# Attention and a maxout layer on one Trainium2 core: W2 Wo accumulated in two halves at the head, and attention moved from two batches ahead to one

## The chip, the cores and the metric

The kernel runs on one core of one Trainium2 chip. The metric is the device time of that core in microseconds (us).

## The reference, cut to what matters

```python
B, H, S, Ns, D = (8, 8, 512, 32, 64)          # d_model 512, d_ff 1024
a      = softmax(scale * x @ state.T)         # 512 tokens attend to 32 states
xread  = a @ state
a2     = softmax(scale * state @ x.T)         # 32 states attend to 512 tokens
sread  = a2 @ x
x      = concat([xread, sread])               # (8 * 544, 512)
out    = maximum(x @ w1, x @ w2) @ w_out
```

The kernels use three identities. `xread @ W` is `a @ (state @ W)`, so each batch multiplies its states into the weights once ("SW") and layer 1 contracts over the states instead of over the model dimension. `max(h1, h2)` is `h2 + relu(h1 - h2)`, so layer 1 needs only W1 - W2 and a ReLU. The term `h2 @ Wo` is `a @ (state @ (W2 Wo))`; so the product W2 Wo (512 x 512) is formed once. In the names of tiles, xt is x transposed, aT is a transposed, sr is the sread of one batch (the "state rows", whose own layers run for all batches near the end; sread_t collects them transposed), r is a ReLU's output and ob a batch's output.

## The kernel before

One batch in the steady loop is layer 1 (16 matmuls and 8 ReLUs), then layer 2 (4 chunks of 10 matmuls); the attention of a later batch is put as "fillers" between the chunks. Slots 8 to 11 are the places behind chunks 0 to 3 of layer 2.

```python
LEAD = 2
xio  = ctx.enter_context(tc.tile_pool(name="xio", bufs=3))
keep = ctx.enter_context(tc.tile_pool(name="keep", bufs=LEAD + 1))
psum = ctx.enter_context(tc.tile_pool(name="ps", bufs=8, space=bass.MemoryType.PSUM))
# ... loads on the SP queue: states, x0, x1, W2 and W1 in halves, x2, states, x3; Wo on GpSimd

def l2(b, fill):
    # ...
    for c in range(NC):
        # ... 10 matmuls into one PSUM bank: 2 with aT (SW), 8 with r (Wo)
        copy("A" if c % 2 else "V", ob[:, c, :], p)
        # ...
        run(*fill.get(NF + c, ()))
    if b < B - 1:
        nc.sync.dma_start(out=dst, in_=ob)          # the 1 MB output, after the last filler

def fillers(b):
    # ...
    n = b + LEAD
    if n < B:
        put(8, lambda: u_sc(n, 0))                  # scores, exp, norm
        put(9, lambda: u_sc(n, 1))
    # ... compact_x(n + 1), u_sw(b + 1)
    if n < B:
        put(10, lambda: u_sr(n))
        put(11, lambda: d_at(n), lambda: u_srt(n))  # d_at: transposing DMA into aT
    if n + 1 < B:
        put(11, lambda: d_xt(n + 1))                # transposing DMA into xt
```

At the head, attention and layer 1 of batches 0 and 1 run interleaved while the weights arrive; W2 Wo comes after them, in one piece:

```python
def w_wo(i):
    p = bank()
    for f in range(NF):
        nc.tensor.matmul(p, w2t[:, i, f, :], wo[:, f, :], start=(f == 0), stop=(f == NF - 1))
    negate("A", wcat[:, i, FF:WC], p)
```

The softmax here doesn't subtract the row's maximum and nothing guards it: scores larger than these inputs give would overflow.

## Time and profile before

| | before |
|---|---|
| time, median of 3 runs | 163.75 us (163.23 to 164.83) |
| span of the profiled run | 161.7 us |
| TensorE (PE) busy | 145.4 us, 90% |
| start of layer 2 of batch 0 | 47.09 us |
| one batch of the loop | 14.32 us |
| mean granted clock of TensorE | 0.996 |

The page's rows of digits cut the span into 40 slices of some 4 us; a digit is the busy share in tenths. The prediction shows those rows, the chain of waits and one batch of the loop. Two further lines of the page are needed later: the granted clock of TensorE by slice, and the group of W2 Wo (busy us, mean ns of one matmul, then PE's idle time ahead of the group).

```profile
PEclk9999999999999999999999999999999999999998
...
L350 PE MATMUL ps<-wo,w2t 128*128 128x512 bf16 x32 | 7.1, 379 | 0.0
```

The first six nines of the clock row are not a measurement: the packed trace (the file that is kept of the profiled run) holds no clock record before 23.96 us, and the page shows time without a record as full. Five warm-up matmuls take 2.31 us there, 0.4 us each or more, against 0.22 for one of W2 Wo, so PE was cold. The mean clocks in the tables suffer from the same and are not compared.

A 512-column matmul is recorded with 379 ns though its successors start every 216 ns: records of matmuls overlap. Hence a gap in brackets before a group is some 0.16 us shorter than the time that PE really lost. Sums of lost time have this 0.16 added for each gap.

### The profile page before, as it was taken

Reading aid. Unit: us, or ns where it says so; the run is one execution under the profiler, and the core shown is the slowest. Engines: PE = TensorE matmul, PEld = TensorE weight load, DVE = VectorE, ACT = ScalarE, POOL = GpSimd, SP = SyncE. Lnnn points to the kernel's source line nnn. Section 1 sums busy time; section 2 is a strip of 40 time slices with the busy share of each in tenths; the row PEclk is TensorE's granted clock in tenths of the full one; section 3 lists DMA queues with packets and bytes.
Section 4 is the critical chain, followed back from the end, with each engine's and each line's share of the span. In section 5 each row is a group of like instructions: output and inputs, shape, how many; then the busy total and the mean of one; then the engine's idle time right before and its main releaser. Section 6 shows DMA issues by size and latency. Waiting matters only on the chain.

```text
span 161.7 us, 3207 instructions
## 1 busy us (share of the span) xinstructions
PE 145.4 (90%) x1349; PEld 72.0 (45%) x1349; DVE 87.0 (54%) x150; ACT 77.9 (48%) x130; POOL 37.1 (23%) x41
## 2 busy tenths in 40 slices
PE   6267389499999999999999999999999999999990
PEld 2255245354544444444445444444444444744430
DVE  5457638799594257355565645556564533416110
ACT  3154955759437166538365743837254243307001
POOL 3140299431002725202702520220130000000000
PEclk9999999999999999999999999999999999999998
DMA  4999999920862796995399096039104400613131
GB/s 111 352 384 386 381 317 196 256 94 2 157 232 47 152 298 225 227 302 191 85 305 303 26 183 271 4 68 315 71 4 130 195 0 4 259 38 92 65 129 67
DMA packets 34365, 27.98 MB, mean 173 GB/s; under 512 B 21424, under 2 KB 30640, under 8 KB 33456
## 3 DMA queue, kind: packets, MB, share of 16 engines
q1 hardware_dynamic: 33312, 26.74, 54.7%
q0 software_dynamic: 1040, 1.05, 4.1%
q8 instruction: 10, 0.16, 0.4%
q14 instruction: 3, 0.02, 0.1%
HBM read 15.20 MB, written 8.91 MB: 149 GB/s over the span
## 4 chain that ended last, share of the span: by engine, by line
PE 85%; DVE 7%; DMA 3%; ACT 2%; issue 1%; SPq 0%
PE ps L292 43%; PE ps L277 17%; PE ps L350 4%; PE ps L239 4%; PE ps L181 3%; DMA xf<-in_x_dram 3%; PE ps L306 2%; PE ps L316 2%; PE ps L204 2%; PE ps L163 2%; PE ps L252 2%; DVE w1b L60 2%; DVE sbd L60 1%; DVE es L188 1%; PE ps L314 1%; PE ps L222 1%
## 5 line engine op out<-in xcount | busy, mean ns | idle before, releaser
L292 PE MATMUL ps<-wo,r 128*128 128x512 bf16 x256 | 60.5, 379 | 0.0
L292 PEld LDWEIGHTS <-r 128*128 128x128 bf16 x256 | 24.8, 98 | 29.7 <-issue 0.4
L267 DVE TENSOR_SCALAR r<-ps 128x512 bf16<-128x512 f32 x32 | 22.1, 691 | 17.3 <-PE ps L277 17.2
L191 POOL TENSOR_TENSOR a<-e,er 128x512 bf16<-128x512 bf16 x14 | 15.1, 1080 | 70.7 <-DVE er L190 35.6
L277 PE MATMUL ps<-aT,swt 128*128 128x512 bf16 x128 | 29.4, 380 | 0.3 <-ACT swt L58 0.3
L58 ACT COPY ob<-ps 128x512 f32<-128x512 f32 x16 | 9.4, 585 | 28.0 <-PE ps L292 24.8
L265 ACT ACTIVATE r<-ps 128x512 bf16<-128x512 f32 x32 | 19.2, 600 | 7.4 <-PE ps L277 7.0
L60 DVE COPY ob<-ps 128x512 f32<-128x512 f32 x16 | 11.1, 692 | 18.7 <-PE ps L292 18.6
L58 ACT CAST swt<-ps 128x512 bf16<-128x512 f32 x24 | 13.9, 588 | 11.8 <-PE ps L239 9.7
L292 PE MATMUL ps<-swt,aT 128*128 128x512 bf16 x64 | 19.1, 382 | 0.3 <-DVE swt L60 0.3
L277 PEld LDWEIGHTS <-swt 128*128 128x128 bf16 x128 | 12.1, 98 | 14.6 <-issue 0.6
L184 ACT ACTIVATE e<-ps 128x512 bf16<-128x512 f32 x16 | 9.6, 600 | 18.4 <-PE ps L181 16.3
L60 DVE CAST swt<-ps 128x512 bf16<-128x512 f32 x24 | 15.7, 661 | 4.9 <-PE ps L252 3.2
L188 DVE TENSOR_REDUCE es<-e 128x16 f32<-128x512 bf16 x16 | 10.9, 682 | 12.4 <-ACT e L184 12.4
L62 POOL CAST xp<-xf 128x2048 bf16<-128x2048 f32 (+1 forms) x9 | 13.6, 1516 | 12.3 <-DMA xf<-in_x_dram 12.2
L58 ACT CAST xc<-xf 128x1024 bf16<-128x1024 f32 x12 | 12.4, 1048 | 0.0
L181 PE MATMUL ps<-sbd,xt 128*128 128x64 bf16 x128 | 7.2, 205 | 2.2 <-ACT xt L58 1.1
L181 PEld LDWEIGHTS <-xt 128*128 128x128 bf16 x128 | 6.2, 105 | 5.8 <-DVE xt L60 1.4
L239 PE MATMUL ps<-wcat,sbd 64*32 64x512 bf16 x160 | 8.1, 386 | 0.0
L292 PEld LDWEIGHTS <-aT 128*128 128x128 bf16 x64 | 4.7, 97 | 7.0 <-issue 3.8
L350 PE MATMUL ps<-wo,w2t 128*128 128x512 bf16 x32 | 7.1, 379 | 0.0
L252 PE MATMUL ps<-w1b,sbd 64*32 64x256 bf16 x64 | 2.6, 338 | 4.4 <-DVE w1b L60 4.4
(60 smaller groups left out, 113.4 us busy)
## 6 DMA issues: line engine op xcount, KB each, us to landing
xf<-in_x_dram SPq DMA_DIRECT2D x7, 1024.0 KB, 7.9
out_dram<-ob SPq DMA_DIRECT2D x7, 1024.0 KB, 4.9
w2f<-in_moe_w_dram SPq DMA_DIRECT2D x2, 1024.0 KB, 11.2
w1f<-in_moe_w_dram SPq DMA_DIRECT2D x2, 1024.0 KB, 12.8
xf<-in_x_dram SPq DMA_DIRECT2D x2, 512.0 KB, 5.0
wo<-in_moe_w_out_dram POOLq DMA_DIRECT2D x1, 1024.0 KB, 12.5
out_dram<-ob SPq DMA_DIRECT2D x4, 256.0 KB, 2.0
out_dram<-obs SPq DMA_DIRECT2D x8, 64.0 KB, 1.7
```

The lines of the kernel that those rows point to most:

```text
L58: nc.scalar.copy(o, i)
L60: nc.vector.tensor_copy(o, i)
L62: nc.gpsimd.tensor_copy(o, i)
L181: nc.tensor.matmul(p[:, k * 64:k * 64 + 64], d["xt"][:, 4 * i + 2 * g + cp, :], sbd[:, b, 2 * i + g].rearrange("p u n -> p (u n)"), start= ...
L188: nc.vector.tensor_reduce(d["es"][:, g], d["e"][:, g].rearrange("p i c n -> p (i c) n"), axis=mybir.AxisListType.X, op=ALU.add)
L191: mul.tensor_mul(d["a"][:, g].rearrange("p c i n -> p i c n"), d["e"][:, g], d["er"][:, g].rearrange("p (i c) -> p i c", i=4).unsqueeze(3) ...
L239: nc.tensor.matmul(pg[g][32 * i:32 * i + 32, :], sbd[64 * g:64 * g + 64, b, 2 * i + g, g, :], wcat[64 * g:64 * g + 64, i, ch * 512:(ch + 1 ...
L265: nc.scalar.activation(out=o, in_=p, func=ACTF.Relu)
L267: nc.vector.tensor_scalar(o, p, scalar1=0.0, scalar2=None, op0=ALU.max)
L277: nc.tensor.matmul(p, SW[b][:, g, f * 128:(f + 1) * 128], AT[b][:, g, :], start=(g == 0), stop=(g == 1))
L292: nc.tensor.matmul(p, w, v, start=(k == 0), stop=(k == NF + 1))
L350: nc.tensor.matmul(p, w2t[:, i, f, :], wo[:, f, :], start=(f == 0), stop=(f == NF - 1))
```

## The change

The intent: form W2 Wo in the head, where PE idles and DMA is full, instead of in the full stretch; make layer 2 of batch 0 in two passes as Wo's halves arrive; and keep less in SBUF and PSUM by running attention one batch ahead. The diff, cut to its core:

```diff
-    LEAD = 2
+    TWO = 3
-    xio = ctx.enter_context(tc.tile_pool(name="xio", bufs=3))
+    xio = ctx.enter_context(tc.tile_pool(name="xio", bufs=2))
-    keep = ctx.enter_context(tc.tile_pool(name="keep", bufs=LEAD + 1))
+    keep = ctx.enter_context(tc.tile_pool(name="keep", bufs=2))
-    psum = ctx.enter_context(tc.tile_pool(name="ps", bufs=8, space=bass.MemoryType.PSUM))
+    psum = ctx.enter_context(tc.tile_pool(name="ps", bufs=4, space=bass.MemoryType.PSUM))
+    accs = ctx.enter_context(tc.tile_pool(name="acc", bufs=4, space=bass.MemoryType.PSUM))
 ... loads
-    load_states(first); load_x(0, 2); load_x(1); W2 and W1 by halves; x2; states; x3
+    load_w(w2f, moe_w2, 0)
+    load_wo(0)
+    load_states(first)
+    load_x(0)
+    load_w(w2f, moe_w2, 1)
+    load_wo(1)
+    load_w(w1f, moe_w1, 0)
+    load_w(w1f, moe_w1, 1)
+    load_x(1)
+    ... the other states; x2
 ... layer 2
+    def l2_close(b, c):
+        copy("A" if c % 2 else "V", ob[:, c, :], OB[b][1 + c])
+        if b == B - 1:
+            nc.sync.dma_start(out=dst[:, c:c + 1], in_=ob[:, c:c + 1])
+        elif c == NC - 1:
+            nc.sync.dma_start(out=dst, in_=ob)
     def l2(b, fill):
         for c in range(NC):
-            ... 10 matmuls and a copy
+            l2_open(b, c)
+            l2_add(b, c, range(NF))
+            l2_close(b, c)
             run(*fill.get(NF + c, ()))
-        if b < B - 1:
-            nc.sync.dma_start(out=dst, in_=ob)
 ... W2 Wo
+    def w_wo(ch, i):
+        if ch == 0:
+            WO[i] = acc()
+        for f in range(4 * ch, 4 * ch + 4):
+            nc.tensor.matmul(WO[i], w2t[:, i, f, :], wo[:, f, :], start=(f == 0), stop=(f == NF - 1))
+        if ch:
+            copy("A" if i % 2 else "V", wcat[:, i, FF:WC], WO[i])
 ... fillers
-        n = b + LEAD
+        n = b + 1
-            put(10, lambda: u_sr(n))
-            put(11, lambda: d_at(n), lambda: u_srt(n))
+            put(10, lambda: u_sr(n), lambda: d_at(n))
+            put(11, lambda: u_srt(n))
 ... head (abridged)
+    warm_up(9); W2 half 1 cast and transposed; Wo half 1 cast; W2 Wo half 1 for rows 0, 1
+    states, their negation, cast of x0; W2 Wo half 1 for rows 2, 3; attention of batch 0
+    W2 half 2 cast and transposed; Wo half 2 cast; W2 Wo half 2 for all rows
+    SW and layer 1 of batch 0; layer 2 of batch 0 over f 0..3, later over f 4..7, batch 1 between
+    state copies and W1 - W2 moved into layer 2 of batch 1
```

The 1 MB output was issued after the last filler, and is now issued inside `l2_close`, ahead of it. The last filler issues the transposing DMA into xt on the same SP queue.

More of the change, by code (lines that the diff above doesn't have):

```diff
@@ L54, in bank, with acc @@
         return psum.tile([128, 512 if dtype == F32 else 1024], dtype, tag="ps", name="ps")
+    def acc():
+        return accs.tile([128, 512], F32, tag="acc", name="acc")
     def copy(eng, o, i):
@@ L86, in load_states, with load_w, load_wo @@
                           in_=state[bs].rearrange("b (q h) n d -> (h n) (b q) d", q=2))
-    first, rest = slice(0, 2), (slice(2, 5), slice(5, 8))
-    load_states(first)
-    load_x(0, 2)
-    load_x(1)
+    first, rest = slice(0, 3), (slice(3, 6), slice(6, 8))
     w2f = stage.tile([128, 4, FF], F32)
     w1f = stage.tile([128, 4, FF], F32)
-    for ch in range(2):
+    wof = stage.tile([128, NF, DM], F32)
+    def load_w(t, w, ch):
         cs = slice(ch * 512, (ch + 1) * 512)
-        nc.sync.dma_start(out=w2f[:, :, cs], in_=moe_w2.rearrange("(i p) f -> p i f", p=128)[:, :, cs])
-        nc.sync.dma_start(out=w1f[:, :, cs], in_=moe_w1.rearrange("(i p) f -> p i f", p=128)[:, :, cs])
+        nc.sync.dma_start(out=t[:, :, cs], in_=w.rearrange("(i p) f -> p i f", p=128)[:, :, cs])
+    def load_wo(ch):
+        nc.sync.dma_start(out=wof[:, 4 * ch:4 * ch + 4],
+                          in_=moe_w_out.rearrange("(k p) n -> p k n", p=128)[:, 4 * ch:4 * ch + 4])
+    load_w(w2f, moe_w2, 0)
[7 more added lines that the diff above has]
+    load_x(1)
+    load_states(slice(3, 8))
     load_x(2)
-    load_states(slice(2, 8))
-    load_x(3)
     ident = consts.tile([128, 128], BF16)
@@ L107 @@
     nc.vector.memset(sbd, 0.0)
+    sneg = consts.tile([128, TWO, 4, Ns], BF16)
     wo = consts.tile([128, NF, DM], BF16)
@@ L110 @@
     w1b = stage.tile([128, 4, FF], BF16)
-    w2n = stage.tile([128, 4, FF], BF16)
+    w2b = stage.tile([128, 4, FF], BF16)
     w2t = stage.tile([128, 4, NF, 128], BF16)
@@ L133, in states @@
                  p[64 * g:64 * g + 64, 0:256 * n].rearrange("p (b h n) -> p b h n", b=n, h=H))
+            if bs.start == 0:
+                negate("A", sneg[64 * g:64 * g + 64],
+                       p[64 * g:64 * g + 64, 0:256 * n].rearrange("p (b i g n) -> p g b i n", b=n, i=4, g=2)[:, g])
     sread_t = consts.tile([128, 4, B * Ns], BF16)
@@ L149, in compact_x @@
         if g == 0:
-            st[b]["xc"] = at.tile([128, H, NC * D], BF16, tag="xc", name="xc")
+            st[b]["xc"] = at.tile([128, H, NC * D], BF16, tag="xc", bufs=1, name="xc")
         copy("A", st[b]["xc"][:, 4 * g:4 * g + 4], xf_t[b][:, 4 * g:4 * g + 4])
@@ L233, with u_sw @@
     swt = consts.tile([128, 2, 2, WC], BF16)
-    def u_sw(b, ch):
+    def u_sw(b, ch, engs="VA"):
         pg = [bank(), bank()]
-        for i in range(4):
-            for g in range(2):
-                nc.tensor.matmul(pg[g][32 * i:32 * i + 32, :], sbd[64 * g:64 * g + 64, b, 2 * i + g, g, :],
-                                 wcat[64 * g:64 * g + 64, i, ch * 512:(ch + 1) * 512],
-                                 start=True, stop=True)
-        for g in range(2):
-            copy("A" if g else "V", SW[b][:, g, ch * 512:(ch + 1) * 512], pg[g])
-    def u_sw01(q, engs):
-        pg = [bank(), bank()]
-        for b in range(2):
-            for k, w in enumerate((w1b, w2n)):
-                for i in range(4):
-                    for g in range(2):
-                        nc.tensor.matmul(pg[g][32 * i:32 * i + 32, b * 256:(b + 1) * 256],
-                                         sbd[64 * g:64 * g + 64, b, 2 * i + g, g, :],
-                                         w[64 * g:64 * g + 64, i, q * 256:(q + 1) * 256],
-                                         start=(b == 0 and k == 0), stop=(b == 1 and k == 1))
-        for g in range(2):
-            copy(engs[g], swt[:, :, g, q * 256:(q + 1) * 256], pg[g].rearrange("p (b w) -> p b w", b=2))
+        two = b < TWO and ch < 2
+        terms = ((sbd, w1b), (sneg, w2b)) if two else ((sbd, wcat),)
+        for k, (sv, w) in enumerate(terms):
+            for i in range(4):
+                for g in range(2):
+                    gs = slice(64 * g, 64 * g + 64)
+                    nc.tensor.matmul(pg[g][32 * i:32 * i + 32, :],
+                                     sneg[gs, b, i, :] if k else sbd[gs, b, 2 * i + g, g, :],
+                                     w[gs, i, ch * 512:(ch + 1) * 512],
+                                     start=(k == 0), stop=(k == len(terms) - 1))
+        for g in range(2):
+            copy(engs[g], SW[b][:, g, ch * 512:(ch + 1) * 512], pg[g])
     flip = [0]
@@ L279, in l1, with l2_open, l2_add @@
             run(*fill.get(f, ()))
+    OB = {}
+    def l2_open(b, c):
+        if c == 0:
+            OB[b] = [big.tile([128, NC, DM], F32, tag="ob", name="ob")] + [None] * NC
+        OB[b][1 + c] = acc()
+        for g in range(2):
+            nc.tensor.matmul(OB[b][1 + c], AT[b][:, g, c * 128:(c + 1) * 128], SW[b][:, g, FF:WC], start=(g == 0), stop=False)
+    def l2_add(b, c, fs):
+        for f in fs:
+            nc.tensor.matmul(OB[b][1 + c], R[b][:, f, c * 128:(c + 1) * 128], wo[:, f, :], start=False, stop=(f == NF - 1))
+    def l2_close(b, c):
+        ob = OB[b][0]
+        dst = out[b * L:b * L + S].rearrange("(p c) n -> p c n", c=NC)
+        copy("A" if c % 2 else "V", ob[:, c, :], OB[b][1 + c])
[3 more added lines that the diff above has]
+            nc.sync.dma_start(out=dst, in_=ob)
     def l2(b, fill):
-        r = R.pop(b)
-        ob = big.tile([128, NC, DM], F32, tag="ob", name="ob")
-        dst = out[b * L:b * L + S].rearrange("(p c) n -> p c n", c=NC)
         for c in range(NC):
-            p = bank()
-            cs = slice(c * 128, (c + 1) * 128)
-            mm = [(AT[b][:, g, cs], SW[b][:, g, FF:WC]) for g in range(2)]
-            rr = [(r[:, f, cs], wo[:, f, :]) for f in range(NF)]
-            mm = rr + mm if b == 0 else mm + rr
-            for k, (w, v) in enumerate(mm):
-                nc.tensor.matmul(p, w, v, start=(k == 0), stop=(k == NF + 1))
-            copy("A" if c % 2 else "V", ob[:, c, :], p)
-            if b == B - 1:
-                nc.sync.dma_start(out=dst[:, c:c + 1], in_=ob[:, c:c + 1])
+            l2_open(b, c)
+            l2_add(b, c, range(NF))
+            l2_close(b, c)
             run(*fill.get(NF + c, ()))
-        if b < B - 1:
-            nc.sync.dma_start(out=dst, in_=ob)
     def moe_sread():
@@ L310, in moe_sread @@
         for t in range(NT // 128):
-            p = bank()
+            p = acc()
             ts = slice(t * 128, (t + 1) * 128)
@@ L325, in w_sub, with w_cast, wo_cast @@
         nc.vector.tensor_sub(wcat[:, :, cs], w1f[:, :, cs], w2f[:, :, cs])
-    def w2_cast(ch, engs):
+    def w_cast(o, w, ch):
         cs = slice(ch * 512, (ch + 1) * 512)
-        for k in range(2):
-            negate(engs[k], w2n[:, 2 * k:2 * k + 2, cs], w2f[:, 2 * k:2 * k + 2, cs])
-    def w1_cast(ch):
-        cs = slice(ch * 512, (ch + 1) * 512)
-        copy("V", w1b[:, 0:2, cs], w1f[:, 0:2, cs])
-        copy("A", w1b[:, 2:4, cs], w1f[:, 2:4, cs])
+        copy("V", o[:, 0:2, cs], w[:, 0:2, cs])
+        copy("A", o[:, 2:4, cs], w[:, 2:4, cs])
+    def wo_cast(ch):
+        for e, k in (("V", slice(0, 2)), ("A", slice(2, 3)), ("P", slice(3, 4))):
+            ks = slice(4 * ch + k.start, 4 * ch + k.stop)
+            copy(e, wo[:, ks], wof[:, ks])
     def w_t(ch, half, eng):
@@ L342, in w_t @@
                 nc.tensor.transpose(p[:, (4 * j + k) * 128:(4 * j + k + 1) * 128],
-                                    w2n[:, 2 * half + j, f * 128:(f + 1) * 128], ident)
+                                    w2b[:, 2 * half + j, f * 128:(f + 1) * 128], ident)
         copy(eng, w2t[:, 2 * half:2 * half + 2, 4 * ch:4 * ch + 4, :].rearrange("p j f t -> p j (f t)"),
              p.rearrange("p (j t) -> p j t", j=2))
-    def w_wo(i):
-        p = bank()
-        for f in range(NF):
-            nc.tensor.matmul(p, w2t[:, i, f, :], wo[:, f, :], start=(f == 0), stop=(f == NF - 1))
-        negate("A", wcat[:, i, FF:WC], p)
+    WO = {}
+    def w_wo(ch, i):
[5 more added lines that the diff above has]
+            copy("A" if i % 2 else "V", wcat[:, i, FF:WC], WO[i])
     def fillers(b):
@@ L366, in fillers @@
             put(9, lambda: compact_x(n + 1, 1))
-        if b + 1 < B:
+        if n < B:
             for ch in range(3):
-                put(8 + ch, lambda ch=ch: u_sw(b + 1, ch))
-        if n < B:
-            put(10, lambda: u_sr(n))
-            put(11, lambda: d_at(n), lambda: u_srt(n))
+                put(8 + ch, lambda ch=ch: u_sw(n, ch))
+            put(10, lambda: u_sr(n), lambda: d_at(n))
+            put(11, lambda: u_srt(n))
         if n + 1 < B:
@@ L378 @@
         SW[b] = swt[:, b % 2]
-    warm_up(5)
-    cast_states(first)
-    states(first)
-    cast_x(0, (("V", slice(0, 4, 2)), ("A", slice(4, 8, 2)), ("P", slice(5, 8, 2))))
-    u_xt(0, 0, "V")
-    copy("V", st[0]["xp"][:, 1:4:2, :, 0:64], xf_t[0][:, 1:4:2].rearrange("p h (c d) -> p h c d", c=NC))
-    u_exp(0, 0)
-    u_xt(0, 1, "A")
-    u_norm(0, 0, nc.vector)
-    u_sc(0, 1, nc.vector)
-    cast_x(1, (("P", slice(0, 4, 2)), ("P", slice(4, 8, 2)), ("A", slice(1, 4, 2)), ("A", slice(5, 8, 2))))
-    u_xt(1, 0, "A")
-    u_at(0, "V")
-    u_xt(1, 1, "V")
-    u_exp(1, 0)
-    u_exp(1, 1)
-    u_sr(0)
-    w2_cast(0, "AA")
-    u_norm(1, 0, nc.gpsimd)
-    u_norm(1, 1, nc.gpsimd)
-    nc.gpsimd.dma_start(out=wo, in_=moe_w_out.rearrange("(k p) n -> p k n", p=128))
-    w2_cast(1, "PP")
-    w1_cast(0)
-    u_srt(0)
-    u_sw01(0, "AV")
-    u_at(1, "A")
-    u_sw01(1, "VA")
-    l1(0, {}, range(0, 2), "VA")
-    l1(1, {}, range(0, 2), "VA")
-    u_sr(1)
-    l1(0, {}, range(2, 4), "VA")
-    l1(1, {}, range(2, 4), "VA")
-    u_srt(1)
+    warm_up(9)
+    w_cast(w2b, w2f, 0)
     w_t(0, 0, "V")
     w_t(0, 1, "A")
-    w1_cast(1)
-    u_sw01(2, "AV")
-    u_sw01(3, "VA")
-    l1(0, {}, range(4, 6), "VA")
-    l1(1, {}, range(4, 6), "VA")
+    wo_cast(0)
+    cast_states(first)
+    w_wo(0, 0)
+    w_wo(0, 1)
+    states(first)
+    cast_x(0, (("V", slice(0, 4, 2)), ("A", slice(4, 8, 2)), ("V", slice(1, 4, 2)), ("P", slice(5, 8, 2))))
+    w_wo(0, 2)
+    w_wo(0, 3)
+    u_xt(0, 0, "V")
+    u_xt(0, 1, "A")
+    u_exp(0, 0)
+    u_exp(0, 1)
+    w_cast(w2b, w2f, 1)
+    u_norm(0, 0, nc.vector)
+    u_norm(0, 1, nc.gpsimd)
     w_t(1, 0, "V")
-    l1(0, {}, range(6, 8), "VA")
-    l1(1, {}, range(6, 8), "VA")
     w_t(1, 1, "A")
+    u_sr(0)
+    u_at(0, "V")
+    u_srt(0)
+    wo_cast(1)
+    w_cast(w1b, w1f, 0)
+    for i in range(4):
+        w_wo(1, i)
+    u_sw(0, 0)
+    u_sw(0, 2)
+    l1(0, {}, range(0, 4))
+    for c in range(NC):
+        l2_open(0, c)
+    w_cast(w1b, w1f, 1)
+    u_sw(0, 1)
+    cast_x(1, (("P", slice(0, 4, 2)), ("P", slice(4, 8, 2)), ("V", slice(1, 4, 2)), ("A", slice(5, 8, 2))))
+    for c in range(NC):
+        l2_add(0, c, range(0, 4))
+    u_xt(1, 0, "V")
+    u_xt(1, 1, "A")
+    l1(0, {}, range(4, 6))
+    u_sc(1, 0, nc.vector)
+    l1(0, {}, range(6, 8))
+    u_sc(1, 1, nc.gpsimd)
     cast_x(2)
@@ L426 @@
     d_xt(2)
-    for bs in rest:
-        cast_states(bs)
-    for q in range(4):
-        w_sub(q)
-    for i in range(4):
-        w_wo(i)
-    for bs in rest:
-        states(bs)
-    u_sw(0, 2)
-    u_sw(1, 2)
-    cast_x(3)
-    load_x(4)
-    l2(0, {8: [lambda: u_sc(2, 0), lambda: compact_x(3, 0), lambda: compact_x(3, 1), lambda: d_xt(3)],
-           9: [lambda: u_sc(2, 1)], 10: [lambda: u_sr(2)], 11: [lambda: d_at(2), lambda: u_srt(2)]})
-    cast_x(4)
-    load_x(5)
-    l2(1, {8: [lambda: u_sc(3, 0), lambda: u_sw(2, 0), lambda: compact_x(4, 0)],
-           9: [lambda: u_sc(3, 1), lambda: u_sw(2, 1), lambda: compact_x(4, 1)],
-           10: [lambda: u_sr(3), lambda: u_sw(2, 2)], 11: [lambda: d_at(3), lambda: u_srt(3), lambda: d_xt(4)]})
-    for b in range(2, B):
-        fill = fillers(b)
-        if b + LEAD + 1 < B:
-            cast_x(b + LEAD + 1)
-            if b + LEAD + 2 < B:
-                load_x(b + LEAD + 2)
+    load_x(3)
+    l2_add(0, 0, range(4, 8))
+    l2_close(0, 0)
+    u_sw(1, 0)
+    l2_add(0, 1, range(4, 8))
+    l2_close(0, 1)
+    u_sw(1, 1)
+    l2_add(0, 2, range(4, 8))
+    l2_close(0, 2)
+    u_at(1, "V")
+    u_sw(1, 2)
+    l2_add(0, 3, range(4, 8))
+    l2_close(0, 3)
+    u_sr(1)
+    u_srt(1)
+    for b in range(1, B):
+        fill = fillers(b)
+        if b + 2 < B:
+            cast_x(b + 2)
+            if b + 3 < B:
+                load_x(b + 3)
+        if b == 1:
+            for bs in rest:
+                cast_states(bs)
+                fill[8].append(lambda bs=bs: states(bs))
+            for q in range(4):
+                fill[8 + q].append(lambda q=q: w_sub(q))
         l1(b, fill)
```

## The prediction

> **What bounds the kernel now.** I read the page's parts 1 and 2, then the chain that ended last, then the time line of each engine over the first 50 us, then one batch in the middle (80 to 95 us).
>
> ```profile
> PE 145.4 (90%) x1349; PEld 72.0 (45%) x1349; DVE 87.0 (54%) x150; ACT 77.9 (48%) x130; POOL 37.1 (23%) x41
> ...
> PE   6267389499999999999999999999999999999990
> DVE  5457638799594257355565645556564533416110
> ...
> DMA  4999999920862796995399096039104400613131
> ```
>
> TensorE is the bound, but only from about 31 us on: its first eight slices (4 us each) hold the idle time, while the DMA engines are full. So a gain can come only from the head, or from less matmul work. The chain of waits by order of time (start, duration, what) splits the two:
>
> ```profile
> 19.78 0.93 DVE w1b L60
> ...
> 29.14 1.73 DVE w1b L60
> ...
> 36.77 6.91 PE ps L350 x32
> 43.68 0.35 PE ps L130 x6
> 44.05 0.55 DVE sbd L60
> ...
> 47.09 0.59 PE ps L292 x2
> ...
> 80.32 3.45 PE ps L277 x16
> ```
>
> W2 Wo (6.91 us, 32 matmuls at 216 ns) runs at 36.8 us on a full PE; the change wants it in the idle head. Layer 2 of batch 0 starts at 47.09, and from there PE runs without a gap to 157.48: 110.4 us. One steady batch takes 94.64 - 80.32 = 14.32 us.
>
> The timeline of the steady batch shows how much slack the transposing DMAs have (SP queue, and the first user of each):
>
> ```profile
> 92.17 1.24 SPq L213 DMA_TRANSPOSE aT<-a  x1
> ...
> 93.50 1.97 SPq L155 DMA_TRANSPOSE xt<-xc  x1
> ...
> 94.62 0.58 ACT L58 COPY ob<-ps 128x512 f32<-128x512 f32 x1 [1.99 <-PE ps L292]
> ...
> 95.56 0.94 SPq L298 DMA_DIRECT2D out_dram<-ob  x1
> ...
> 100.09 0.40 PE L181 MATMUL ps<-sbd,xt 128*128 128x64 bf16 x8
> ```
>
> and part 6 gives issue to landing:
>
> ```profile
> out_dram<-ob SPq DMA_DIRECT2D x7, 1024.0 KB, 4.9
> ```
>
> The transpose into xt takes 4.3 to 4.5 us from issue to landing (the view of that tile), so it lands at 97.9 and PE reaches its user at 99.87: 2.0 us of slack. The transpose into aT takes 2.7 and lands at 94.87.
>
> **What the Trainium skill says.** (1) "DMA: Bandwidth & Descriptors", section "Queues, rings and completion order": on each DMA engine the descriptors of a ring are consumed in order. The trace agrees: xt's transpose lands 4.4 us after issue although the 1 MB output follows 2 us behind, the same fine windows show 213 GB/s until 97 us and only then some 400 GB/s, and the output, which takes 3.9 us alone (issued at 123.86), takes 4.9 behind the transpose. (2) "TensorE: Matmul & The Clock Gate", Part 1: TensorE has a cold and a warm clock, matmuls of 512 columns are 426.7 ns apart cold and 215.7 ns warm, and warmth needs some 3.4 us of sustained work. The trace agrees: five warm-up matmuls take 2.31 us, eight 64-column ones 0.61 us at 8.2 us and 0.23 at 47.7, W2 Wo 216 ns each. (3) "PSUM — Partial Sum Buffer", Terms: two engines on one bank and quadrant at once is an error. The trace of before has no such pair; in the new kernel's instruction list VectorE's copies into sbd and ScalarE's into sneg, of one bank, wait for one another in turn. (4) "SBUF — State Buffer", section "SBUF: two separate sides": VectorE in a 2-port mode and GpSimd lock one another out. Agrees: the w1b cast takes 0.93 us alone and 1.73 beside a GpSimd cast at 28.2.
>
> **Part 1: the head.** Loads first. From the windows of one microsecond, 0.44 MB arrive by 4 us and then about 0.375 MB/us, and a transfer lands about 1.25 us after its last byte (x's first half: 0.655 MB are in at 4.6, its user starts at 5.88). With the new order and a slightly better start for the first block (2 KB rows) that gives landings: W2 half 1 at 6.3, Wo half 1 at 9.1, states 10.3, x0 13.1, W2 half 2 15.9, Wo half 2 18.7, W1 halves 21.5 and 24.3, x1 27.1, x2 31.4. Before, x0's halves landed at 5.9 and 7.3.
>
> Then the engines, each in the order of its instruction list, with durations from before's rows: W2 cast 1.0 us on two engines, to 7.3; transposes and their copies (0.69 on VectorE, 1.01 on ScalarE) to 10.15; Wo cast to 10.05 (its ScalarE slice to 10.75). W2 Wo for rows 0 and 1 from 10.1: 8 matmuls, 3.4 us cold or 1.7 warm. Behind them on PE stand the state transposes, then four copies that take turns (two of 0.55, two of about 0.45, plus semaphores, 2.2 us): 14.3 to 16.5 cold. VectorE, in order, can cast x0 only after these: 16.9, though x0 landed at 13.1. Then the known chain: x0 transposes and copies to 19.4, exps to 20.6, norms to 22.7 and on GpSimd to 23.8, aT to 25.1, Wo half 2 cast 26.0, W1 cast 26.95. So the second half of W2 Wo starts at 26 (cold) or 24 (warm), not when Wo lands (18.7): VectorE's queue holds it, not the loads. From there to layer 1 of batch 1, PE has (warm): 3.45 (W2 Wo) + 1.5 (three SW groups) + 1.7 + 1.7 (half of layer 1, the opening matmuls) + 3.45 + 1.0 (transposes) + 1.7 + 0.5 + 3.45 + 1.5 + 0.85 = 20.8 us, and waits: 1.7 cold matmuls, 0.7 for SW copies, about 1.5 for the last ReLU behind the norm on VectorE, 0.6 for sr. Layer 1 of batch 1 starts at 48 to 52; I take 50.5.
>
> Remaining from there: 110.4 - 8.66 (layer 2 of batch 0 done) + 3.45 (layer 1 of batch 1 not done) + 0.6 (10 state transposes) + 0.4 (second terms of batch 2's SW) = 106.2 us. 50.5 + 106.2 = 156.7 against 157.5: **the head as such gains only about 1 us**; the matmul work hidden is paid back by attention of batch 0 coming later, with VectorE in its path.
>
> **Part 2: layer 2 of batch 1.** Four state copies (2.26 us) and four subtractions (4.62) move into it. VectorE's list there adds up to about 12.5 us against PE's 11; it delays the second norm, hence aT of batch 2, and the first ReLUs of batch 2: **1.5 us**.
>
> **Part 3: one batch ahead.** The slots of the fillers do not move in the steady loop, so aT lands at 94.87 where layer 1 wants it at 94.64: 0.3 us. More important is the order on the SP queue, which the instruction lists show: before, aT, xt, output; after, aT, output, xt, because the output is now issued before the last filler. The output cannot be issued before its last copy (94.62 + 0.58): 95.27, for 0.94; xt's transpose is then issued at 96.25 instead of 93.5. The output's data run about 96.1 to 98.6; the transpose's 2.4 us stand behind them, to 101.0, and land 0.7 later: 101.7 where PE wants xt at 99.87. That is **1.8 us per batch**, and it contains the 0.3. It hits xt of batches 3 to 7; the first is partly hidden in Part 2's delay: 4 x 1.8 + 0.5 = 7.7 us. Four PSUM banks instead of eight for the rest do not bind: layer 1 fills a bank every 0.43 us and each is free 1.3 us later, so four (1.73) suffice.
>
> **Sum.** 156.7 + 1.5 + 7.7 = 165.9 for the end of PE, 8.4 above 157.5; tail unchanged. 163.75 + 8.4 = **172 us**.
>
> **Rivals.** (a) The head wins: warm all through from the nine warm-up matmuls and no waits, layer 1 of batch 1 at 44.4 (23.6 + 20.8). That is 6 us less: 166. For it: W2 Wo really leaves the full stretch. Against: VectorE's order, and PE's cold clock up to 24 us in the trace of before. (b) Descriptors are not strictly in order, or the transpose overlaps the output: then only the later issue (2.75 us against 2.0 of slack) remains, 0.75 per batch, 3.5 us in all: 168. (a) and (b) together: 162, "same" or a little faster. (c) The queue is worse than FIFO (transpose descriptors made slower under a full ring, as the 5.7 and 7.3 us issues at 10 to 24 us hint), or the VectorE pile in layer 2 of batch 1 costs 3 us: 177.
>
> **Range and chances.** The head is uncertain by about 2.5 us, the transposes by as much: 166 to 177. Faster by over 2% (under 160.5) needs more than (a) and (b) together: 0.05. Within 2%: 0.15. Slower: 0.80.
>
> **What would show it.** Right: PE idle ahead of the first score matmuls of batches 3 to 7, released by the DMA into xt, 1 to 2 us each, with a batch period near 16 us and the transposes landing 5 us or more after issue; the output before xt on SP's timeline. Right for the head: the second half of W2 Wo starting at 24 to 26 us, behind VectorE. Wrong: a period of 14.3 us (no stall), or layer 1 of batch 1 before 46 us. The prediction fails if the descriptors interleave, or if PE is warm from 5 us on.

## The result, and the profile after

| | before | after |
|---|---|---|
| time, median (all runs) | 164.29 us (163.23 to 164.88, 4 runs) | 175.61 us (175.45 to 177.34, 4 runs) |
| ratio of after to before, 95% interval | | 1.072 (1.064 to 1.080): slower |
| span of the profiled run | 161.7 us | 175.6 us |
| layer 1 of batch 1 starts | | 52.77 us |
| one batch of the loop | 14.32 us | 16.33, 16.55, 16.36 us |
| mean granted clock | 0.996 | 0.949 |

A ratio is the mean time of one kernel's fast runs over that of the other's of the same rounds, so not quite the ratio of the quoted medians. The profiled run of after is the slowest of its four, 177.34 us.

The page of the kernel after, busy digits and three groups of matmuls (busy us, mean ns, idle before and its main releaser):

```profile
PE 151.2 (86%) x1305; PEld 70.0 (40%) x1305; DVE 90.1 (51%) x158; ACT 78.2 (45%) x130; POOL 32.8 (19%) x40
...
PE   7378569999689997999879987989798979899991
...
PEclk9858955999999999999999999999999999999999
...
L287 PE MATMUL ps<-aT,swt 128*128 128x512 bf16 x128 | 29.6, 379 | 3.0 <-ACT ob L62 2.3
...
L373 PE MATMUL acc<-wo,w2t 128*128 128x512 bf16 x32 | 12.1, 552 | 3.4 <-DVE wo L64 3.4
...
L200 PE MATMUL ps<-sbd,xt 128*128 128x64 bf16 x128 | 6.4, 194 | 5.5 <-DMA xt<-xc 4.7
```

PE is no longer full in the loop: the row of nines of before has a 7 or an 8 in each batch. The score matmuls (L200) wait 4.7 us in all for the DMA into xt, and layer 1 (L287) has its own waits. W2 Wo takes 12.1 us instead of 7.1, with 552 ns a matmul instead of 379, and the clock row shows the reason: 5 to 8 tenths in the slices in which it runs.

The order on the SP queue, one batch (start, us to issue, what):

```profile
82.12 1.24 SPq L232 DMA_TRANSPOSE aT<-a  x1
85.23 0.35 SPq L311 DMA_DIRECT2D out_dram<-ob  x1
85.64 4.77 SPq L174 DMA_TRANSPOSE xt<-xc  x1
```

The output goes first now, and the transpose behind it takes 4.77 us to be issued where it took 1.97. It lands 6.4 to 6.6 us after its start in the loop, instead of 4.3 to 4.5. PE in the same batch:

```profile
85.23 3.63 PE L287 MATMUL ps<-aT,swt 128*128 128x512 bf16 x16 [0.59 <-ACT ob L62]
...
92.12 0.41 PE L200 MATMUL ps<-sbd,xt 128*128 128x64 bf16 x8 [1.10 <-DMA xt<-xc]
...
101.56 3.63 PE L287 MATMUL ps<-aT,swt 128*128 128x512 bf16 x16 [0.57 <-ACT ob L62]
```

Two waits a batch: one ahead of layer 1, one ahead of the scores. With the 0.16 us each they make 0.75 + 1.26 = 2.01 us, which is 16.33 - 14.32.

The head, in the timeline of PE:

```profile
10.04 3.57 PE L373 MATMUL acc<-wo,w2t 128*128 128x512 bf16 x8 [2.09 <-DVE wo L64]
...
25.44 6.53 PE L373 MATMUL acc<-wo,w2t 128*128 128x512 bf16 x16 [1.27 <-DVE wo L64]
...
52.77 3.62 PE L287 MATMUL ps<-aT,swt 128*128 128x512 bf16 x16
```

The second half of W2 Wo waits for VectorE's cast of Wo until 25.44, and then all its 16 matmuls run slow: 6.5 us where 16 warm ones start over 3.5.

### The profile page after: what moved, and what is told of

It reads as the page before. It is cut to its first block, busy times and chain, and to the rows that moved or that the text cites. A ratio compares the mean times of both kernels' runs of the same rounds, so it can differ in the third digit from the quotient of the medians.

```text
span 175.6 us, 3119 instructions
## 1 busy us (share of the span) xinstructions
PE 151.2 (86%) x1305; PEld 70.0 (40%) x1305; DVE 90.1 (51%) x158; ACT 78.2 (45%) x130; POOL 32.8 (19%) x40
## 5 line engine op out<-in xcount | busy, mean ns | idle before, releaser
L302 PE MATMUL acc<-wo,r 128*128 128x512 bf16 x256 | 60.9, 379 | 1.4 <-DVE r L277 1.4
L287 PE MATMUL ps<-aT,swt 128*128 128x512 bf16 x128 | 29.6, 379 | 3.0 <-ACT ob L62 2.3
L62 ACT COPY ob<-acc 128x512 f32<-128x512 f32 x16 | 9.4, 586 | 25.3 <-PE acc L302 23.8
L287 PEld LDWEIGHTS <-swt 128*128 128x128 bf16 x128 | 11.9, 98 | 18.1 <-DMA aT<-a 3.9
L64 DVE COPY ob<-acc 128x512 f32<-128x512 f32 x16 | 11.0, 687 | 15.1 <-PE acc L302 15.1
L298 PE MATMUL acc<-swt,aT 128*128 128x512 bf16 x64 | 18.7, 382 | 0.0
L66 POOL CAST xp<-xf 128x2048 bf16<-128x2048 f32 (+1 forms) x9 | 14.1, 1569 | 9.7 <-DMA xf<-in_x_dram 9.7
L373 PE MATMUL acc<-wo,w2t 128*128 128x512 bf16 x32 | 12.1, 552 | 3.4 <-DVE wo L64 3.4
L200 PE MATMUL ps<-sbd,xt 128*128 128x64 bf16 x128 | 6.4, 194 | 5.5 <-DMA xt<-xc 4.7
L200 PEld LDWEIGHTS <-xt 128*128 128x128 bf16 x128 | 5.3, 98 | 10.3 <-DMA xt<-xc 7.2
L373 PEld LDWEIGHTS <-w2t 128*128 128x128 bf16 x32 | 4.2, 132 | 10.1 <-issue 9.0
```

The lines of the kernel that those rows point to most:

```text
L62: nc.scalar.copy(o, i)
L64: nc.vector.tensor_copy(o, i)
L66: nc.gpsimd.tensor_copy(o, i)
L200: nc.tensor.matmul(p[:, k * 64:k * 64 + 64], d["xt"][:, 4 * i + 2 * g + cp, :], sbd[:, b, 2 * i + g].rearrange("p u n -> p (u n)"), start= ...
L287: nc.tensor.matmul(p, SW[b][:, g, f * 128:(f + 1) * 128], AT[b][:, g, :], start=(g == 0), stop=(g == 1))
L298: nc.tensor.matmul(OB[b][1 + c], AT[b][:, g, c * 128:(c + 1) * 128], SW[b][:, g, FF:WC], start=(g == 0), stop=False)
```

## The experiments

Two theories stood after the first look. The main one: the loop loses time because the output was put ahead of xt's transpose on one queue, plus a smaller part by slots that are too late for aT; the head gains nothing because its matmuls run cold. The rival: attention one batch ahead (with two buffers and four PSUM banks) is itself too tight, or the head is what costs.

### a1: the output issued last again

```diff
-        elif c == NC - 1:
+        elif c == NC - 1 and b == 0:
             nc.sync.dma_start(out=dst, in_=ob)
     def l2(b, fill):
         ...
             run(*fill.get(NF + c, ()))
+        if b < B - 1:
+            nc.sync.dma_start(out=out[...], in_=OB[b][0])
```

> The changed kernel, but in the loop the output of a batch is issued after the last filler, so that the SP queue has aT, xt, output again. Theory (xt stands behind the output): xt lands some 4.4 us after issue instead of 6.4, the 1.1 to 1.5 us waits ahead of the score matmuls of batches 4 to 7 (5.3 us in all) go, aT's 0.75 us waits stay or shrink a little; 175.6 falls to about 170, ratio to the kernel before about 1.04. Rival (xt is late because attention runs only one batch ahead, whatever the queue order): no change, 175.

Measured: 171.41 us, ratio 1.046 (1.039 to 1.053). The waits ahead of the scores of batches 4 to 7 are gone, and in the loop xt lands after 4.3 to 4.4 us. SP and PE of one batch:

```profile
82.26 1.60 SPq L174 DMA_TRANSPOSE xt<-xc  x1
84.08 1.10 SPq L320 DMA_DIRECT2D out_dram<-ob  x1
```

```profile
84.28 3.63 PE L287 MATMUL ps<-aT,swt 128*128 128x512 bf16 x16 [0.80 <-DMA aT<-a]
```

So the order on the queue caused the waits for xt. It gives back 4.2 us of the 11.3 by the medians. The wait ahead of layer 1 stays. In two of four batches the profile now names aT's transpose instead of ScalarE's copy of the output, in the other two ScalarE's copy into sread_t; each of these ends at nearly the same time as aT's landing, so the name alone decides nothing.

### a2: a1, and aT transposed by PE

```diff
-            put(10, lambda: u_sr(n), lambda: d_at(n))
+            put(10, lambda: u_sr(n), lambda: u_at(n, "V"))
```

> As the run with the output issued last, and aT made by eight PE transposes and a VectorE copy in slot 10 instead of the transposing DMA. Theory: the 0.75 us waits ahead of layer 1 (batches 3 to 6) go and 0.45 us of PE work per batch comes in their place; period about 14.8 us, total about 168.5 to 169.5. If the wait ahead of layer 1 was really for ScalarE's copy of the output chunk, it stays and the total is above the run before it.

Measured: 170.78 us, ratio 1.041 (1.035 to 1.047). In the steady loop no wait is left ahead of layer 1 and the batch takes 14.76 us, so it was the DMA into aT that released PE. The total improved by only 0.6 us, less than expected: six batches pay some 0.45 us each for the transposes on PE (14.76 - 14.32), 2.7 us against some 3.8 us of waits removed (4.3 in a1, of which 0.5 stayed). A fix that costs work on the bound engine is hardly a fix.

### b1: in the kernel before, only the output moved ahead

```diff
             if b == B - 1:
                 nc.sync.dma_start(out=dst[:, c:c + 1], in_=ob[:, c:c + 1])
+            elif c == NC - 1:
+                nc.sync.dma_start(out=dst, in_=ob)
             run(*fill.get(NF + c, ()))
-        if b < B - 1:
-            nc.sync.dma_start(out=dst, in_=ob)
```

> The kernel before, with two batches of lead, but the output issued ahead of the last filler's two transposes. Theory (queue order alone makes the wait): xt of batches 4 to 7 lands 7 us or more after the output's issue, waits of 2 to 3 us each ahead of four score matmuls, 8 to 12 us in all: 172 to 176. Rival (it is the shorter lead): the order costs nothing here, 164.

Measured: 184.68 us, ratio 1.126 (1.119 to 1.133). The order alone is enough to slow the kernel before, and by more than expected. PE in one batch:

```profile
75.09 0.41 PE L181 MATMUL ps<-sbd,xt 128*128 128x64 bf16 x8 [2.98 <-DMA xt<-xc]
...
76.21 3.22 PE L292 MATMUL ps<-wo,r 128*128 128x512 bf16 x8
```

Here aT's transpose also stands behind the output, and xt's behind both: a wait of 2.93 to 2.98 us, four times. That explains 12.5 us of the 20.8 (11.9 in the brackets, and 0.16 for each). After the wait eight matmuls take 3.22 us instead of 1.89. The windows of 1 us say why (us, then busy time of PE, PEld, DVE, ACT, POOL, then the granted clock, the DMA share and GB/s):

```profile
77.00:78.00 1.00, 1.00 (x4) 0.36 (x3) 0.80 (x2) 0.61 (x2) 0.60 (x1) 0.50 0.97 345
78.00:79.00 1.00, 1.00 (x4) 0.40 (x3) 0.00 (x0) 0.00 (x0) 0.45 (x1) 0.50 0.14 46
```

The granted clock is 0.50 there, and about four matmuls fit in a microsecond. A wait of 3 us costs the wait and then some matmuls at half speed. The trace has some 16 us at half clock outside the waits, in four stretches; half of that, some 8 us (an estimate), makes up the rest of the 20.8. The waits of after, 1.3 us, do not have this sequel: its clock row is full in the loop.

### h1: the kernel after with a warm head

Warm-up matmuls fill the idle places: 17 instead of 9 at the start, 9 behind the first cast of Wo, 5 between the transposes of W2's second half, 6 behind the second cast of Wo.

```diff
-    warm_up(9)
+    warm_up(17)
 ...
     wo_cast(0)
+    warm_up(9)
 ...
     w_t(1, 0, "V")
+    warm_up(5)
     w_t(1, 1, "A")
 ...
     wo_cast(1)
+    warm_up(6)
```

> The changed kernel with 28 more warm-up matmuls that fill PE's idle stretches of the head (8 more at the start, 9 ahead of the first half of W2 Wo, 5 between the W2 transposes, 6 ahead of the second half). Theory (the 32 W2 Wo matmuls cost 12.1 us instead of 6.9 because PE's clock was cold): mean of that row from 552 to about 380 ns, layer 1 of batch 1 starts 3 to 5 us earlier, 175.6 falls to 171 to 172.5. Rival (VectorE's queue sets the head): the clock is warm and the total hardly falls, 174.5 or more.

Measured: 185.14 us, ratio 1.129 (1.122 to 1.136), far off. The head did what was expected; the group of W2 Wo and the start of layer 1 of batch 1 are

```profile
L373 PE MATMUL acc<-wo,w2t 128*128 128x512 bf16 x31 | 7.2, 378 | 0.5 <-DVE wo L64 0.4
```

```profile
47.81 3.62 PE L287 MATMUL ps<-aT,swt 128*128 128x512 bf16 x15
```

so W2 Wo is 4.9 us shorter and the loop starts 5.0 us sooner than in the profiled run of after. (Five other profiled runs, a1, a2, s1, p1 and p2, have after's head with its cold clock, two of them with 28 tiny matmuls more, and start the loop at 50.8 to 52.0; against them it is 3 to 4 us.) But the loop lost more: the waits for xt are now 2.10, 2.61, 2.91, 2.61 and 3.17 us, and behind three of them (2.10, 2.61 and 2.61) PE runs at half clock for 3.4 us, as in b1. Nothing in the loop's program differs between after and h1. This asked for an explanation of its own.

PE's instructions themselves come by DMA: the page lists 10 packets, 0.16 MB in all, on a queue of kind "instruction", so 16 KB each. (That they are PE's is inferred, from the count that follows.) The Trainium skill, "Runtime: NRT & Kernel Launch", section "Instruction fetch mechanics", says that an engine's instructions are fetched in blocks of 16 KiB, 256 instructions, while it runs. The trace agrees on the size. One batch is 129 matmuls and 129 weight loads, 258 instructions, so the fetch should fall at nearly the same place of each batch, and it does: in after the packets start in the half-microsecond windows at 78.5, 95.0, 111.5, 126.5 and 142.5 us. Additional instructions ahead of the loop shift that place. In h1 the packets are at 70.5, 90.0, 109.5, 127.5 and 147.0, each in the last 2.5 us of a wait for xt.

### p1: the kernel after with 28 tiny matmuls ahead of the loop

h1 adds 28 matmuls. p1 adds 28 of 16 columns, which shift the instruction stream by as much but leave the head cold.

```diff
     warm_up(9)
+    pt = bank()
+    for k in range(28):
+        nc.tensor.matmul(pt[:, 0:16], warm[:, 0:128], warm[:, 0:16], start=(k == 0), stop=(k == 27))
```

> The changed kernel with 28 matmuls of only 16 columns put into PE's idle time behind the nine warm-ups: as many PE instructions more as in the run with 28 more warm-ups, but hardly any more work, so the clock of the head stays about as cold as in the changed kernel. Theory (the loss of the warm run comes from where PE's instruction fetch falls in the batch, one 16 KB packet per batch, and not from warmth): the waits ahead of the score matmuls grow to 2.1 to 3.2 us here too, each with an instruction packet some 2.3 us before its end, and the time is 182 to 188. Rival (warmth, or the earlier head itself, makes the transposes late): waits of 1.1 to 1.5 us, 175 to 176.

Measured: 188.92 us, ratio 1.149 (1.141 to 1.156). The head stays as in after (W2 Wo 545 ns a matmul, layer 1 of batch 1 at 52.02), the waits for xt become 2.1 to 2.9 us, and every other batch has half clock behind the wait. 28 matmuls of no work at the start cost 13.3 us in the loop: its waits for xt add up to 14.1 us instead of 5.6, and three stretches of 3.4 us at half clock cost some 5 us more (an estimate: half of them). So what lengthens the waits is the place of the instruction fetch, or something else that moves with the number of PE instructions, but not the warmth of the head.

### h2: h1 with each warm-up matmul split into two of 256 columns

```diff
-        for k in range(n):
-            nc.tensor.matmul(p, warm[:, 0:128], warm, ...)
+        for k in range(2 * n):
+            nc.tensor.matmul(p[:, 0:256], warm[:, 0:128], warm[:, 0:256], ...)
```

> The warm run with each warm-up matmul of 512 columns replaced by two of 256: the same warmth, but 65 PE instruction pairs more than in the changed kernel instead of 28, which moves the instruction fetch by about half a batch against the changed kernel. Theory (fetch phase): the waits ahead of the score matmuls are 1.1 to 1.5 us again, the head's gain of 4.9 us stays, and the time is 170 to 172. Rival (warmth): 185 as in the warm run.

Measured: 172.21 us, ratio 1.048 (1.044 to 1.053). The same warm head (layer 1 of batch 1 at 48.07) with another phase of the stream: 13 us below h1. The waits for xt fall to 0.2 to 0.6 us, below the 1.1 to 1.5 expected, but those for aT rise to 1.2 to 1.6: the packets now come some 3 us ahead of the end of those. (xt still lands 6.4 to 6.6 us after its issue; PE, held by aT, comes later to it.) The four kernels beside one another, packets again by half-microsecond windows:

| kernel | packets of PE's instructions at | that is | waits for xt | waits for aT | time |
|---|---|---|---|---|---|
| after | 95.0, 111.5 | in no wait | 1.1 to 1.3 us | 0.6 us | 175.61 |
| h1 | 90.0, 109.5 | some 2 us before a wait for xt ends (92.29, 111.88) | 2.1 to 3.2 us | not longer | 185.14 |
| p1 | 94.0, 131.5 | some 2 us before a wait for xt ends (96.52, 133.98) | 2.1 to 2.9 us | not longer | 188.92 |
| h2 | 94.5, 111.0 | some 3 us before a wait for aT ends (97.50, 113.96) | 0.2 to 0.6 us | 1.2 to 1.6 us | 172.21 |

How the fetch lengthens a wait can be read from the traces. The DMA view of h1 by 1 us windows shows the small packets of xt's transpose, issued at 103.82, thin out in the window that starts at 109 (queue and kind: packets, MB, share of 16 engines):

```profile
q1 hardware_dynamic: 541, 0.14, 71.9%
q8 instruction: 1, 0.02, 6.0%
```

In the next window there are 126 packets of about 1 KB, those of the next load; in after the same change comes equally long, some 6 us, after the issue. Yet PE goes on 8.1 us after the issue in h1 and 6.7 in after:

```profile
111.88 0.41 PE L200 MATMUL ps<-sbd,xt 128*128 128x64 bf16 x8 [2.91 <-DMA xt<-xc]
```

The traces also record when a transfer's completion was signalled: each of these transposes adds 16 to a semaphore in steps of one. The view of xt's tile gives the time to the last step, in after and in h1:

```profile
DMA to landing us min/median/max: 6.3/6.4/6.6
DMA to landing us min/median/max: 4.9/8.0/8.4
```

For the transpose issued at 103.82, the packed trace has fifteen steps between 110.16 and 110.38 and the sixteenth at 111.84; PE starts 0.04 us later. So PE waits for the data and not for its own instructions: one part in sixteen is 1.5 us late. In all twelve traces, 14 transposes into xt had an instruction packet start some 2 us ahead of their landing (five in h1, five in p1, one each in after, a1, a2 and s1). In 13 of them fifteen steps came at the usual time and the last 1.5 to 1.6 us behind; in the other all sixteen were late. Where no packet fell into a transpose, its steps lie within 0.3 us of one another. In h2 the packets fall into aT's transposes, 0.7 to 0.9 us after the issue, and five of these land after 3.7 to 4.0 us instead of 3.0 (a sixth, with its packet 0.2 us after the issue, lands after 3.0). So an instruction packet that falls into a transpose delays it, and the wait grows by that. That the late part is the one on the DMA engine that carries the packet is likely but not shown: the trace kept does not tell the engine.

### p2 and b2: the same tiny matmuls where there is no wait for xt

p2 is a1 with the 28 tiny matmuls of p1:

```diff
     warm_up(9)
+    (the 28 tiny matmuls)
 ...
-        elif c == NC - 1:
+        elif c == NC - 1 and b == 0:
 ... and the output after the fillers, as in a1
```

> The 28 tiny matmuls and, in the loop, the output issued last. Theory (the instruction fetch only hurts where PE stands waiting behind the output and the transposes): with the output last there is no wait for xt for it to lengthen, so about 171 to 172 as in the run with the output last alone. Rival (28 more PE instructions cost by themselves): some 13 us more than that, 184.

Measured: 171.89 us, ratio 1.048 (1.040 to 1.056), as a1 (1.046).

b2 is the kernel before with them:

```diff
     warm_up(5)
+    (the 28 tiny matmuls)
     cast_states(first)
```

> The kernel before with the same 28 tiny matmuls behind its warm-ups. Theory: its loop has no waits for transposes, so where the fetch falls does not matter: 164 to 165.5 (the tiny matmuls add up to 1 us to the head). Rival: sensitive as well, 170 or more.

Measured: 164.49 us, ratio 1.001 (0.994 to 1.009): the same. So 28 more instructions cost nothing by themselves. That a packet inside a transpose would be harmless in these two kernels is not shown: in neither trace does one fall into a transpose of the loop.

### s1: a1, with attention one slot earlier

```diff
-            put(8, lambda: u_sc(n, 0))
-            put(9, lambda: u_sc(n, 1))
+            put(7, lambda: u_sc(n, 0))
+            put(8, lambda: u_sc(n, 1))
 ...
-            put(10, lambda: u_sr(n), lambda: d_at(n))
-            put(11, lambda: u_srt(n))
+            put(9, lambda: u_sr(n), lambda: d_at(n))
+            put(10, lambda: u_srt(n))
 ...
-            put(11, lambda: d_xt(n + 1))
+            put(10, lambda: d_xt(n + 1))
```

> The run with the output issued last, and the next batch's score matmuls one filler slot earlier (slots 7 and 8), aT's transpose in slot 9, xt's in slot 10. Theory (with one batch of lead both transposes only need some 2 us more): no waits ahead of layer 1 nor of the score matmuls, period 14.3 to 14.5 us, and the wait ahead of the state rows' layer goes; 171.4 falls by 4 x 0.8 + 0.8 to about 167. What is left above the kernel before (about 3 us) is then the head. Rival (one batch of lead cannot be hidden): a wait of another kind, for VectorE or a PSUM bank, period still above 15, 170 or more.

Measured: 165.76 us, ratio 1.011 (1.005 to 1.017): the same within 2%. Layer 1 of two successive batches, without a wait ahead of either:

```profile
82.01 3.62 PE L287 MATMUL ps<-aT,swt 128*128 128x512 bf16 x16
...
96.33 3.62 PE L287 MATMUL ps<-aT,swt 128*128 128x512 bf16 x16
```

The batch takes 14.32 us again. So one batch of lead, two buffers and four PSUM banks cost nothing in the loop, and the rival falls. The 9.9 us between after and s1 agree with the waits of after in the loop and before the state rows, 8.8 + 0.95. The 1 us left is put down to what precedes the steady loop, the head and a wait of 0.92 us for a ReLU of batch 2; it was not split.

### v2: s1 with a warm head

v2 adds h1's warm-ups to s1, and takes three things out of VectorE's and ScalarE's way: the negation of the states comes after the cast of x0; half of W1 - W2 moves from layer 2 of batch 1 into the head; and batch 1's norm goes to GpSimd. One SW block of batch 1 also comes earlier.

```diff
+    (the warm-up matmuls of h1)
-    states(first)
-    cast_x(0, ...)
+    neg = states(first)
+    cast_x(0, ...)
+    neg()
 ...
     u_sw(0, 1)
     cast_x(1, ...)
+    w_sub(0)
+    w_sub(1)
 ...
-    u_sc(1, 0, nc.vector)
+    u_sc(1, 0, nc.gpsimd)
     u_sc(1, 1, nc.gpsimd)
+    u_sw(1, 0)
 ... (and not a second time behind l2_close(0, 0))
```

> An attempt to beat both: the slots run with the 28 warm-ups, the sneg copies after the x0 casts on ScalarE, two of the four W1 - W2 subtractions in VectorE's idle time of the head, and the last ReLU of batch 0 freed from the norm on VectorE. Theory: the head's cold clock (5 us), VectorE's turn with sneg (1 us), the last ReLU (1.4) and the pile in layer 2 of batch 1 (1.5) are what the head lost; 158 to 161 against 164 before. If the instruction fetch still falls badly, 165 or more in spite of a head that is 6 us or more earlier.

Measured: 158.64 us (158.46 to 158.83), ratio 0.965 (0.962 to 0.969): faster than both kernels. Its page:

```profile
PE 148.8 (95%) x1333; PEld 70.4 (45%) x1333; DVE 90.1 (57%) x157; ACT 78.0 (50%) x130; POOL 34.0 (22%) x41
...
PEclk9999999999999999999999999999999999999999
...
L377 PE MATMUL acc<-wo,w2t 128*128 128x512 bf16 x32 | 7.4, 379 | 0.4 <-DVE wo L64 0.4
```

PE is busy 95% of the span, W2 Wo is warm, layer 1 of batch 1 starts at 45.47 (52.77 in after), and the batch takes 14.32 us. The stream has the same 28 additional matmuls as h1 and p1, and no harm comes of them: no packet falls into a transpose of the loop in this trace, and no wait for xt is left. Which of the two protects it was not tested. How much each of the pieces in the head gave was not measured singly.

All runs of the experiments are recorded as correct. In short:

| kernel | median us | ratio to before |
|---|---|---|
| after | 175.61 | 1.072 |
| a1: after, output last | 171.41 | 1.046 |
| a2: a1, aT on PE | 170.78 | 1.041 |
| b1: before, output first | 184.68 | 1.126 |
| h1: after, warm head | 185.14 | 1.129 |
| p1: after, 28 tiny matmuls | 188.92 | 1.149 |
| h2: h1, warm-ups halved | 172.21 | 1.048 |
| p2: a1, 28 tiny matmuls | 171.89 | 1.048 |
| b2: before, 28 tiny matmuls | 164.49 | 1.001 |
| s1: a1, attention a slot earlier | 165.76 | 1.011 |
| v2: s1, warm head and eased VectorE | 158.64 | 0.965 |

## Why the prediction was right or wrong

The direction was right and for the predicted reason: 172 was predicted with a range of 166 to 177, the median is 175.6. The sum was 6.1 us short in the profiled run (177.34, the slowest), so it was the width of the range that held the median; and within Part 3 two errors partly cancelled, which was luck. The terms of its sum against the profiled run:

| term | predicted | measured |
|---|---|---|
| layer 1 of batch 1 starts | 50.5 (48 to 52) | 52.77 |
| PE's work from there on, without waits | 106.2 | 107.9 |
| Part 2, layer 2 of batch 1 | 1.5 | 1.05 for sr + 0.42 for a ReLU = 1.5 |
| Part 3, waits for xt and aT | 7.7 | 5.6 for xt + 3.3 for aT = 8.8 |
| wait of the state rows for the last sread_t | none | 0.95 |
| end of PE | 165.9 | 171.97 |

(Measured work is 171.97 - 52.77 less the waits of 11.26.)

- **The head, Part 1.** The mechanism was right: the second half of W2 Wo starts at 25.44, within 24 to 26, behind VectorE's cast of Wo and not behind the load. The landings of the first six loads were right too, within 0.4 us. Mis-sized was the cold clock: the sum held 1.7 us for it, but all 16 matmuls of the second half ran cold, and from their start to that of the next group are 6.46 us instead of the 3.45 of warm ones, 3.0 us lost. That is 1.3 of the 2.3 us by which layer 1 of batch 1 was late; the waits from there on were right (2.75 against 2.8), and the last 1 us is 0.2 in the start of the second half and some 0.8 of work, not traced. W2 Wo as a whole lost 12.1 - 7.1 = 5.0 us against the kernel before; h1 takes them away by warmth alone. Rival (a), the head wins, did not come about in after; v2 shows that it could be had.
- **Work left.** The sum subtracted 8.66 us for layer 2 of batch 0 from what follows 47.09 us in before. But 8 of its 40 matmuls, 1.73 us, had been run before 47.09 there (at 44.90). That is the 1.7 us of this row, an error of bookkeeping.
- **Part 2** was right in size and in the engine, VectorE, with its state copies and subtractions. But PE waited for sr (0.90 us in brackets), which stands behind them in VectorE's list, more than for aT of batch 2 and a ReLU, so the agreement to 0.1 us is in part luck.
- **Part 3.** Right: the output ahead of xt on the SP queue, waits of 1.3 to 1.5 us for batches 4 to 7 with a period near 16, and the first of the five (0.28 us) hidden. a1 shows the cause by taking it away. Wrong in two details, of opposite sign: the waits for xt were 2.1 us smaller than the 7.7 of the sum, and those for aT, 3.3 us, were not in it. The step "and it contains the 0.3" failed: aT landed after 3.0 us instead of 2.7 and its wait, 0.75 us a batch, came in addition; a1 keeps it, and s1 removes it by an earlier slot. And the transpose was held longer on SP, 4.77 us against the 1.97 assumed, though its own wait at PE was smaller than 1.8.
- **Rival (b)**, that the transpose overlaps the output, is refuted by the landing of 6.4 us and by a1. **Rival (c)**, a queue that is worse than in order, is partly what the 4.77 us show.
- **Missed.** The last batch's sread_t is now made just ahead of the state rows, which wait 0.95 us for it. And nothing in the prediction foresaw that a wait for xt can double with the number of instructions ahead of it. In after no instruction packet happened to fall into a transpose of the loop, which was luck; the same change with 28 more matmuls measured 189, outside the range. One reading of the prediction compares unlike things: the eight 64-column matmuls take 0.61 us at 8 us in PE's timeline, and 0.40 there at 47.5; 0.23 is what the chain has left of them after the overlap with the matmul before.

## What to carry to other kernels

On an in-order DMA queue, issue the small transfer that the bound engine waits for ahead of the large output, and compare each filler's lead with the time from issue to landing before pulling it nearer to its use. Moving matmuls into an idle head pays only when the engine is warm there and the casts that feed them are not queued behind something else: here the same idea was 7% slower as written and 3.5% faster with the order, the slots, the clock and VectorE's list repaired. Where PE waits for a transposing DMA, changes of no work (28 tiny matmuls) moved the time by 7.6%, because they moved an instruction packet into the transpose; so look where these packets fall before judging a head's change.

## What the Trainium skill lacked or had wrong

- "DMA: Bandwidth & Descriptors" tells of ring order, but not that a transposing DMA's issue is held on the issuing queue behind a large transfer: 4.77 us instead of 1.97 behind a 1 MB output, and 6.4 us to landing instead of 4.4.
- "Runtime: NRT & Kernel Launch", section "Instruction fetch mechanics", calls the cost of crossing a block "mostly hidden". Where no packet fell into a transpose that held: in the kernel before (1.001 with 28 tiny matmuls) and with the output last (171.9 against 171.4). Where packets fell into xt's transposes, these landed after 7.9 to 8.4 us instead of 6.4 to 6.6, and the same shift went with 13.3 us more (175.6 to 188.9). No page of the skill was found that tells of it.
- "TensorE: Matmul & The Clock Gate", Part 1, puts the penalty of the ramp below 1% of a typical span. Here PE fell back to half clock twice within the head (7.5 to 14.3 us and 21.1 to 31.4 us in after), and cold W2 Wo alone cost 5.0 us of 175.6 (2.8%).
- The same Part 1 lets the clock fall after an idle window of some 3.4 us. Here waits of some 3 us in b1, and of 2.1 us in h1, were followed by half clock (b1: eight matmuls in 3.22 us instead of 1.89), while in h1 waits of 2.9 and 3.2 us were not.
- The same Part 1 warns that recorded clock events can be unreliable, but not that they can be missing at the start: in the kernel before the first record is at 23.96 us, and the page of the profile shows full clock from the first slice, while five warm-up matmuls took 2.31 us and eight 64-column ones 0.61 us at 8 us against 0.40 later.
